# The first MLP matmul of seven chunks as seven half-size products, with g folded into w1, x's block sums on GpSimd and v cast by DMA into its operand

## The chip, the cores and the metric

The kernel runs on one core of a Trainium2 chip. The metric is the device time of one execution in microseconds (us); lower is better. The engines are named as in the profile: PE (TensorE, matmuls), PEld (its weight loads), DVE (VectorE), ACT (ScalarE), POOL (GpSimd), SP (SyncE, which here only issues DMAs).

## What is computed

Linear attention over 8 batches of 8 heads, 576 rows and 64 columns, followed by a layer norm and a two-layer MLP with a residual. Cut to what matters:

```python
q_s = softmax(q, axis=-1)              # over the 64 columns of a head
k_s = softmax(k, axis=2)               # over the 576 rows
kv  = einsum('bhsd,bhse->bhde', k_s, v)
x   = einsum('bhsd,bhde->bhse', q_s, kv)   # heads side by side: (8, 576, 512)
xn  = (x - mean(x)) / sqrt(var(x) + 1e-6) * g_ln
out = x + relu(xn @ w_ch1) @ w_ch2     # w_ch1 512 x 2048, w_ch2 2048 x 512
```

All inputs and the output are float32.

## The kernel before

**Chunks.** The 4608 rows are worked off as nine chunks of 512. Chunks 0 to 7 hold rows 0 to 511 of each batch; chunk 8 (`C9`) holds the last 64 rows of all eight batches. For one chunk, PE computes `mm1` (xn times w1, 2048 hidden columns, then relu into `hT`) and `mm2` (`hT` times w2).

**Order.** The program is in a manual schedule: each engine executes its instructions in the order in which the Python code issues them. `run(main, side)` (L677) walks the matmul steps of a chunk's MLP, each with a weight, and issues a side job as soon as the sum of the weights has reached the job's position. So everything that belongs to the next chunks (attention, exponentials, loads, transposes) has a position within the current chunk: 120 units in chunks 2 to 7 (64 for mm1, 56 for mm2).

**mm1.** `mlp_steps` (L648) gives a chunk above 1 first 32 matmuls of 256 columns (`mm1_part`, L429: the first four blocks of w1, for one half of the chunk's rows and then the other), then 48 matmuls of 512 columns (`mm1`, L414). A block of 128 hidden columns needs four matmuls, one for each 128 of the 512 input columns (`KO1` = 4). ACT applies the relu from PSUM into `hT` (L402, L439).

**mm2** of chunks 1 to 8 (`mm2_fast`, L598) is already computed as seven half-size products: both operands are cut into 2 x 2 blocks and combined by sums and differences. `sum_h` (L494, instructions at L505, DVE) forms four sums S of hT's blocks (`hs`) in two groups; `quarter_w2` (L481, DVE) formed four differences T of w2's blocks (`w2_q`) in chunks 0 and 1. Each product is 16 matmuls of 256 columns (`prod`, L521). Partial results stay in PSUM banks `a`, `b`, `c`, `e`: ACT copies one (`copy_u`, `seed_c`, L546, L619), DVE adds one (`add_u`, L549). `y_quarter` (L532, DVE) scales by the row's 1/sigma and adds the residual, and POOL's DMA queue stores the result (L538).

**PSUM.** Pool `mm_ps` has six banks for all of mm1 and mm2; pool `att_ps` has two for attention. A new tile takes the bank that was released longest ago in program order, and its first writer waits for the last reader of the old tile.

**Attention of the next chunk** (`attn_fast`, L744) lies within the current one: `reduce_q` (L199) sums the exponentials of q; `kv_mm` (L259, 20 short matmuls) multiplies exp(k) with v, with a column of ones beside every pair of heads for the denominator; DVE normalises into `kv_sb` (L268); `po_mm` (L291, 16 short matmuls) gives x. `x_fast` (L338) scales x and accumulates its row sum, L344 turns the sum into minus the mean, and `xn_out` (L331) computes (x - mean) times g, with g in a tile that is repeated over all partitions. ACT's `square_sum` (L325) gives the variance, which is applied only at the end (`rstd_op`). `xn_T` (L207) transposes two quarters of xn by a DMA from SP's queue into `xnT`, mm1's moving operand: quarters 0 and 1 first, quarters 2 and 3 at position 101 of 120.

**Preparation** (`prep_fast`, L731): two chunks ahead, SP's queue loads q, k, v (1 MB each, in runs of 1 KB), and ACT computes the exponentials (L183, L149). v arrives as float32 and is cast by ACT into `vm` (L157) for batches 3 to 7; for batches 1 and 2 the DMA casts it to bf16 and DVE copies it (L159). The last 64 rows go to `vtr` and are cast by DVE into `vr` (L166). POOL's queue has the weights and the first loads at the start, and the stores from then on.

Chunk 8's attention (`attn_rest`) lies in chunk 7. Its MLP comes last, with `last_products` in place of `mm2_fast`'s list, and nothing beside it.

Of the kernel before, what the change touches and what calls it, by code (L numbers as in the profile page):

```python
# [20 lines left out]
def kernel(  # L21
# [30 lines left out]
    VW = P + 2  # L52
# [7 lines left out]
    const = ctx.enter_context(tc.tile_pool(name="const", bufs=1))  # L60
    raw = ctx.enter_context(tc.tile_pool(name="raw", bufs=2))
# [18 lines left out]
    w1_sb = const.tile([P, KO1, DH], BF16)  # L80
# [4 lines left out]
    vr = const.tile([P, 2, NP, VW], BF16)  # L85
    vm = const.tile([P, 2, T, NP, VW], BF16)

# [19 lines left out]
    def alloc_kv(b):  # L107
        raws[b][0], raws[b][1], raws[b][3], raws[b][4] = (
            raw.tile([P, H, T, D], FP32, tag="kt", name="kt", bufs=1),
            raw.tile([P, H, T, D], BF16 if b in CAST else FP32, tag="vt", name="vt", bufs=1),  # L110
            raw.tile([P, H // 2, D], FP32, tag="ktr", name="ktr"),
            raw.tile([P, H // 2, D], FP32, tag="vtr", name="vtr"),
        )
# [8 lines left out]
    def load_kvrem(eng, b):  # L122
        for src, dst in ((k, raws[b][3]), (v, raws[b][4])):
            for half in range(2):
                eng.dma_start(
                    dst[SR * half : SR * half + SR],
                    src[b, 4 * half : 4 * half + 4, SM:S, :].transpose([1, 0, 2]),
                )
# [13 lines left out]
    eks, eqs, eqTs, xs, xnTs, rstds = {}, {}, {}, {}, {}, {}  # L142

    def exp_k(b, j, hn=2):
        kt = raws[b][0]
        if j == 0:
            eks[b] = att.tile([P, T, H, D], BF16, tag="ek", name="ek")
        hs = slice(2 * j, 2 * j + hn)
        nc.scalar.activation(  # L149
            eks[b][:, :, hs, :].rearrange("p t h d -> p h t d"), kt[:, hs], AF.Exp  # L150
        )

    def cast_v(b, j, eng=None):
        hs = slice(2 * j, 2 * j + 2)
        dst = vm[:, b % 2, :, j, 0:P].rearrange("p t (h d) -> p h t d", h=2)
        if eng is nc.scalar:
            nc.scalar.copy(dst, raws[b][1][:, hs])  # L157
        else:
            nc.vector.tensor_copy(out=dst, in_=raws[b][1][:, hs])  # L159

    def prep_kvrem(b):
        par = b % 2
        nc.scalar.activation(ekr[:, par], raws[b][3], AF.Exp)
        for half in range(2):
            ps = slice(SR * half, SR * half + SR)
            nc.vector.tensor_copy(  # L166
                out=vr[ps, par, 2 * half : 2 * half + 2, 0:P],
                in_=raws[b][4][ps].rearrange("p (j h) d -> p j (h d)", h=2),
            )

    def new_eq(c):
        eqs[c] = (
            att.tile([P, T, H, D], BF16, tag="eq", name="eq"),
# [24 lines left out]
    def reduce_q(c, t):  # L198
        nc.vector.reduce_sum(eqs[c][1][:, t], eqs[c][0][:, t], axis=AX.X)  # L199
# [19 lines left out]
    def exp_k0(j):  # L219
        hs = slice(2 * j, 2 * j + 2)  # L220
        if j == 0:
            eks[0] = raw.tile([P, T0, H, D], BF16, tag="vt", name="ek0", bufs=1)
# [23 lines left out]
    def kv_mm(b, j, t):  # L246
# [5 lines left out]
        w = P + 1  # L252
        if b == 0:
            lhsT, rhs, w = k0_mm(j, t)
        elif t < T:
            lhsT, rhs = eks[b][:, t, 2 * j : 2 * j + 2, :], vm[:, par, t, j, 0 : P + 1]
        else:
            lhsT, rhs = ekr[:, par, 2 * (j % 2) : 2 * (j % 2) + 2, :], vr[:, par, j, 0 : P + 1]
# [4 lines left out]
        if j % 2 == 1 and t == last:  # L263
            js = slice(j - 1, j + 1)
            rzk = recip_z(pkv[:, :, P]) if b else kvbox["rz", j // 2]
            for half in range(2):
                ps = slice(64 * half, 64 * half + 64)
                nc.vector.tensor_mul(  # L268
                    kv_sb[ps, b, js, ps], pkv[ps, :, ps],
# [3 lines left out]
    def start_x(c):  # L273
# [3 lines left out]
            mlp.tile([P, T, DM], BF16, tag="xn", name="xn"),  # L277
# [45 lines left out]
    def square_sum(c, t):  # L323
        x, _, _, mv = xs[c]
        nc.scalar.activation(  # L325
            scrap, x[:, t], AF.Square, bias=mv[:, t, 0:1], accum_out=mv[:, t, 1:2]
        )

    def xn_out(c, t):
        x, _, xn, mv = xs[c]  # L330
# [4 lines left out]
    def x_fast(c, t):  # L335
# [6 lines left out]
            accum_out=st[:, t, 0:1],  # L342
        )
        nc.vector.tensor_scalar_mul(out=mv[:, t, 0:1], in0=st[:, t, 0:1], scalar1=-1.0 / DM)  # L344
        xn_out(c, t)

    def x_rest(t):
# [3 lines left out]
            scrap, x[:, t], AF.Copy, scale=-1.0 / DM, accum_out=mv[:, t, 0:1]  # L351
# [37 lines left out]
    def rstd_op(c):  # L389
# [4 lines left out]
            lnv, mv[:, :, 1], AF.Ln, bias=eps_ln, scale=1.0 / DM  # L394
# [14 lines left out]
    def mm1(c, m, ko):  # L409
        if m == 0 and ko == 0:  # L410
            new_h()
        if ko == 0:
            hbox["ph"] = mm_ps.tile([P, T, P], FP32, tag="m", name="ph")
        nc.tensor.matmul(  # L414
            hbox["ph"], w1_sb[:, ko, m * P : (m + 1) * P], xnTs[c][:, :, ko, :],
# [5 lines left out]
    def mm1_part(c, m, t0, tn, ko):  # L421
# [4 lines left out]
        if m % 2 == 0 and at == 0 and ko == 0:  # L426
# [3 lines left out]
            ph[:, m % 2, at : at + tn], w1_sb[:, ko, m * P : (m + 1) * P],  # L430
# [120 lines left out]
    def last_products(product):  # L551
# [32 lines left out]
        product(1, "a", first=True, at={  # L584
# [13 lines left out]
    def mm2_fast(c):  # L598
# [3 lines left out]
        def product(n, name, first=False, at=None, ts=range(2), own=False):  # L602
            at = at or {}
            for t in ts:
                for k in range(KH):
                    i = t * KH + k

                    def go(t=t, k=k, i=i):
                        if i == 0 and first:
                            bank(name)  # L610
                        prod(n, name, t, k, first or own, own)
                        for fn in at.get(i, []):
                            fn()

                    steps.append((0.5, go))
# [16 lines left out]
        def sums(*which):  # L632
            return [lambda g=g, i=i: sum_h(g, i) for g, i in which if g or c == FAST]

        late = c == FAST
        product(1, "a", first=True, at={
            0: sums((1, 0), (0, 1), (1, 1)) + ([] if late else sums((1, 2), (1, 3))), 15: [seed_c]})
        product(5, "b", first=True, at={8: sums((0, 2), (1, 2)) if late else []})
        product(6, "a", at={8: sums((0, 3), (1, 3)) if late else [], 15: [lambda: copy_u("s2")]})
# [7 lines left out]

    def mlp_steps(c):  # L648
        full = range(KO2)
# [4 lines left out]
        else:  # L654
            full, parts = range(4, KO2), ((0, 0, 2), (0, 2, 2))
            if c == 1:
                full, parts = range(8, KO2), ((0, 0, 2), (1, 0, 2), (0, 2, 2), (1, 2, 2))
# [39 lines left out]
    def prep_side(b, a0, a1, sums=True):  # L697

        n = a1 - a0
        s = spread([lambda j=j: exp_q(b, j) for j in range(NP)], a0, a0 + 0.4 * n)  # L700
        s += [(a0 + 0.4 * n, lambda: (prep_kvrem(b), eq_T(b)))]
        s += spread([lambda j=j: exp_k(b, j) for j in range(NP)], a0 + 0.5 * n, a1)
        s += spread([lambda j=j: cast_v(b, j) for j in range(NP)], a0 + 0.1 * n, a0 + 0.5 * n)
        if sums:
            s += spread([lambda t=t: sum_q(b, t) for t in range(T)], a0 + 0.5 * n, a1)
        return s

    def attn_side(c, kv0, kv1, po0, po1, pe=None):


        s = []
        if c < B:
            s += spread(
                [lambda j=j, t=t: kv_mm(c, j, t) for j in range(NP) for t in range(T + 1)],
                kv0, kv1,
            )
        fns = []
        for t in range(T):
            fns += [lambda t=t, i=i: po_mm(c, t, i) for i in range(NP - 1)]
            fns.append(lambda t=t: (po_mm(c, t, NP - 1), x_out(c, t)))  # L720
        s += [(po0, lambda: start_x(c))] + spread(fns, po0, po1)
        if pe:
# [339 lines left out]
```

## Time and profile before

| what | value |
|---|---|
| median of 3 runs | 280.28 us (280.23 to 280.35) |
| span of the profiled execution, first to last instruction | 279.2 us |
| PE busy in it | 273.3 us |
| DVE, ACT, POOL busy | 195.2, 181.9, 36.8 us |
| DMA moved | 48.01 MB in 68844 packets |
| granted clock of PE | full in every slice |
| idle of PE between 60 us and 270 us | none that the table of windows shows |

The page gives the profiled execution by its span alone; the runs' times are about 1.1 us above it (280.28 - 279.2 = 1.08), the part ahead of the first instruction and behind the last. The chain of waits is read from its end backwards: each piece is what had to end for the next one to start. Busy times of DVE and ACT are unions: where two instructions overlap by their pipelines, the time counts once. A single ACT or DVE instruction on 512 columns is recorded with some 0.6 to 0.7 us, and back to back they start some 0.5 to 0.6 us apart.

### The profile page before, as it was taken

Reading aid. Unit: us, or ns where it says so; the run is one execution under the profiler, and the core shown is the slowest. Engines: PE = TensorE matmul, PEld = TensorE weight load, DVE = VectorE, ACT = ScalarE, POOL = GpSimd, SP = SyncE. Lnnn points to the kernel's source line nnn. Section 1 sums busy time; section 2 is a strip of 40 time slices with the busy share of each in tenths; the row PEclk is TensorE's granted clock in tenths of the full one; section 3 lists DMA queues with packets and bytes.
Section 4 is the critical chain, followed back from the end, with each engine's and each line's share of the span. In section 5 each row is a group of like instructions: output and inputs, shape, how many; then the busy total and the mean of one; then the engine's idle time right before and its main releaser. Section 6 shows DMA issues by size and latency. Waiting matters only on the chain.

```text
span 279.2 us, 5666 instructions
## 1 busy us (share of the span) xinstructions
PE 273.3 (98%) x2245; PEld 202.1 (72%) x2245; DVE 195.2 (70%) x457; ACT 181.9 (65%) x346; POOL 36.8 (13%) x64
## 2 busy tenths in 40 slices
PE   8999999999999999999999999999999999999994
PEld 6888855766995589558955896589658855885683
DVE  4573647987996688658865886588657929962363
ACT  4568871797987785678668766876585477526500
POOL 3922224200030003000300030003000300030000
PEclk9999999999999999999999999999999999999999
DMA  7999999799969995994499469544914410241014
GB/s 182 245 207 207 336 218 332 172 256 308 193 155 348 285 173 156 320 230 90 132 328 238 95 146 290 133 75 121 219 38 79 126 65 1 40 122 66 2 38 113
DMA packets 68844, 48.01 MB, mean 172 GB/s; under 512 B 40401, under 2 KB 65489, under 8 KB 68818
## 3 DMA queue, kind: packets, MB, share of 16 engines
q1 hardware_dynamic: 57074, 27.66, 42.7%
q0 software_dynamic: 11152, 19.47, 27.7%
q10 hardware_dynamic: 592, 0.52, 0.6%
q8 instruction: 17, 0.28, 0.4%
q14 instruction: 9, 0.07, 0.1%
HBM read 36.70 MB, written 9.44 MB: 165 GB/s over the span
## 4 chain that ended last, share of the span: by engine, by line
PE 90%; DMA 5%; DVE 2%; POOL 1%; issue 0%; DVEq 0%
PE ph L414 28%; PE ba L521 20%; PE ph L429 15%; PE bb L521 5%; PE bc L521 5%; PE be L521 5%; PE pc L474 4%; DMA w_sb<-in_moe_w_ch_dram 4%; PE pkv L259 3%; PE po L291 2%; DMA qt<-in_q_dram 2%; PE ptr L803 1%; PE po L298 1%; DVE xn L331 1%; POOL v L866 1%; DVE x L338 1%
## 5 line engine op out<-in xcount | busy, mean ns | idle before, releaser
L414 PE MATMUL ph<-xnT,w_sb 128*128 128x512 bf16 x368 | 87.2, 379 | 0.0
L402 ACT ACTIVATE hT<-ph 128x512 bf16<-128x512 f32 x92 | 53.5, 598 | 18.4 <-PE ph L414 18.4
L414 PEld LDWEIGHTS <-w_sb 128*128 128x128 bf16 x368 | 34.0, 98 | 34.5 <-issue 0.2
L521 PEld LDWEIGHTS <-hs 128*128 128x128 bf16 x512 | 49.1, 98 | 5.8 <-DVE hs L505 0.2
L429 PE MATMUL ph<-xnT,w_sb 128*128 128x256 bf16 (+1 forms) x432 | 52.7, 269 | 0.3 <-DMA w_sb<-in_moe_w_ch_dram 0.3
L439 ACT ACTIVATE hT<-ph 128x512 bf16<-128x512 f32 x48 | 28.6, 600 | 24.5 <-PE ph L429 24.3
L429 PEld LDWEIGHTS <-w_sb 128*128 128x128 bf16 x432 | 38.4, 98 | 4.3 <-DMA w_sb<-in_moe_w_ch_dram 0.5
L505 DVE TENSOR_TENSOR hs<-hT 128x1024 bf16<-128x1024 bf16 x32 | 21.9, 687 | 27.8 <-ACT hT L402 27.6
L521 PEld LDWEIGHTS <-hT 128*128 128x128 bf16 x384 | 36.6, 98 | 5.2 <-ACT hT L402 0.2
L538 POOL DMA_DIRECT2D out_dram<-ot x28 | 15.0, 541 | 179.8 <-DVE ot L532 155.9
L521 PE MATMUL ba<-w_q,hs 128*128 128x256 bf16 x256 | 31.3, 273 | 0.0
L331 DVE SCALAR_TENSOR_TENSOR xn<-x,mv,g_bc 128x512 bf16<-128x512 bf16 x34 | 25.5, 751 | 1.2
L338 DVE SCALAR_TENSOR_TENSOR x<-po,rq 128x512 bf16<-128x512 f32 x30 | 20.6, 686 | 6.5 <-PE po L291 6.1
L325 ACT ACTIVATE scrap<-x,mv 128x512 bf16<-128x512 bf16 x34 | 24.6, 724 | 0.1
L291 PE MATMUL po<-kv_sb,eqT 128*128 128x128 bf16 x128 | 24.1, 219 | 0.2 <-DVE kv_sb L268 0.2
L199 DVE TENSOR_REDUCE zq<-eq 128x8 f32<-128x512 bf16 x32 | 20.1, 686 | 4.1 <-ACT eq L191 2.4
L259 PE MATMUL pkv<-vm,ek 128*128 128x129 bf16 x112 | 21.2, 220 | 0.0
L546 ACT COPY s<-ba 128x512 f32<-128x512 f32 x15 | 8.8, 584 | 16.7 <-PE ba L521 16.7
L291 PEld LDWEIGHTS <-eqT 128*128 128x128 bf16 x128 | 11.7, 98 | 7.5 <-issue 0.6
L521 PE MATMUL ba<-w_sb,hT 128*128 128x256 bf16 x128 | 16.2, 273 | 0.0
L474 PE MATMUL pc<-w_sb,hT 128*128 128x512 bf16 x64 | 15.9, 379 | 0.0
L521 PE MATMUL bb<-w_q,hs 128*128 128x256 bf16 x128 | 15.8, 273 | 0.0
(117 smaller groups left out, 340.2 us busy)
## 6 DMA issues: line engine op xcount, KB each, us to landing
out_dram<-ot POOLq DMA_DIRECT2D x32, 256.0 KB, 3.0
qt<-in_q_dram SPq DMA_DIRECT2D x5, 1024.0 KB, 7.5
kt<-in_k_dram SPq DMA_DIRECT2D x5, 1024.0 KB, 6.9
vt<-in_v_dram SPq DMA_DIRECT2D x5, 1024.0 KB, 10.9
w_sb<-in_moe_w_ch_dram POOLq DMA_DIRECT2D x8, 512.0 KB, 14.0
qt<-in_q_dram POOLq DMA_DIRECT2D x2, 1024.0 KB, 15.9
kt<-in_k_dram POOLq DMA_DIRECT2D x2, 1024.0 KB, 15.9
kt<-in_k_dram SPq DMA_DIRECT2D x4, 288.0 KB, 5.9
```

Source lines behind the costliest of these rows:

```text
L259: nc.tensor.matmul(pkv[:, j % 2, 0:w], lhsT, rhs, start=(t == 0 and j % 2 == 0), stop=(t == last), skip_group_check=True,)
L291: nc.tensor.matmul(pobox["p"][:, i * P : i * P + P], eqTs[c][:, t, i, :], kv_sb[:, c, i, :], start=True, stop=True,)
L325: nc.scalar.activation(scrap, x[:, t], AF.Square, bias=mv[:, t, 0:1], accum_out=mv[:, t, 1:2])
L331: nc.vector.scalar_tensor_tensor(xn[:, t], in0=x[:, t], scalar=mv[:, t, 0:1], in1=g_bc, op0=ALU.add, op1=ALU.mult)
L338: nc.vector.scalar_tensor_tensor(x[:, t].rearrange("p (h d) -> p h d", h=H), in0=pobox[c, t].rearrange("p (h d) -> p h d", h=H), scalar=1. ...
L402: nc.scalar.activation(dst, src, AF.Relu)
L414: nc.tensor.matmul(hbox["ph"], w1_sb[:, ko, m * P : (m + 1) * P], xnTs[c][:, :, ko, :], start=(ko == 0), stop=(ko == KO1 - 1),)
L429: nc.tensor.matmul(ph[:, m % 2, at : at + tn], w1_sb[:, ko, m * P : (m + 1) * P], xnTs[c][:, t0 : t0 + tn, ko, :], start=(ko == 0), stop=( ...
L439: nc.scalar.activation(dst, ph, AF.Relu)
L474: nc.tensor.matmul(hbox["pc", t], hbox["h"][:, ko, t, :], w2_sb[:, ko, :], start=(ko == 0), stop=(ko == KO2 - 1),)
L505: nc.vector.tensor_tensor(out=dst, in0=x, in1=y, op=op)
L521: nc.tensor.matmul(hbox[bank][:, t], lhsT, rhs, start=first and (own or t == 0) and k == 0, stop=k == KH - 1, skip_group_check=True)
```

## The change

Seven parts go together.

1. **mm1 of chunks 2 to 8 (`c > FAST`) as seven products** (`mm1_fast`, `prod1`, new). w1's and xn's blocks are cut 2 x 2 (even and odd blocks of 128 hidden columns by two halves of the input columns; two halves of the rows). For each of four groups of four hidden blocks, seven products of four matmuls of 256 columns replace eight. Partial results go through PSUM tiles `x`, `b`, `c`: ACT copies two (`seed`, `copy_5`), DVE adds two (`add_5`, `out_22`), ACT applies three relus, and DVE takes the maximum with zero for the fourth block in SBUF, for two groups at once. The groups go in pairs, slot by slot.
2. **g folded into w1**: `scale_w1` (DVE, eight instructions in chunk 0) writes `w1g` = w1 times g; chunks 1 to 8 use it. g as a column comes from four tiny matmuls and one DVE instruction in `first_batch`. `xn_out` becomes a tensor_scalar of 512 x minus the row sum, without g and without L344; the factor 512 is taken out again in `square_sum` and `rstd_op`. Chunk 0 keeps the old form.
3. **w1's block sums**: `sum_w1` (DVE, sixteen instructions of 128 x 512) in chunks 0 and 1, into the memory of the raw w1.
4. **x's block sums**: `sum_x`, eight instructions of 128 x 256 for each chunk, on POOL for chunks 2 to 7 and on DVE for chunk 8; they need both halves of `xnT`.
5. **v**: for batches 3 to 7 `load_v` issues from POOL's queue four casting DMAs straight into `vm` (runs of 64 numbers: 256 bytes read, 128 written) and two into `vr`. `vm` gets a column of ones beside every head instead of every pair. Casts L157 and L166 go. Batches 1 and 2 keep a staged tile.
6. **Buffers**: `ek` and `eq` have one buffer instead of two; the first batch's `ek` lies in `kt`'s memory.
7. **Positions**: a chunk above 1 has 112 units now (56 and 56), and nearly every side job is moved: exponentials and square sums lie in mm2, kv_mm at 4 to 28, po_mm at 48 to 75, the second `xn_T` at 78, `sum_x` at 84 to 100, `reduce_q` in two double-size instructions within the chunk before. In mm2, some products take their matmuls in another order (`cut`).

```diff
+    def load_v(b):
...
+        for t in range(0 if b in CAST else T):
+            nc.gpsimd.dma_start(vm[:, b % 2, t, :, 0:D], src[:, t])
...
+    def sum_x(c, i):
...
+        dst, x, y = ((t1, b12, b11), (t2, b22, t1), (t3, b22, b12), (t4, b21, t2))[i]
+        eng = nc.gpsimd if c < C9 else nc.vector
+        for t in range(2):
+            eng.tensor_tensor(out=dst[:, t], in0=x[:, t], in1=y[:, t], op=ALU.subtract)
...
     def xn_out(c, t):
+        nc.vector.tensor_scalar(
+            out=xn[:, t], in0=x[:, t], scalar1=float(DM), scalar2=mv[:, t, 0:1],
+            op0=ALU.mult, op1=ALU.subtract,
+        )
...
+    def mm1_fast(c):
...
+        def seed(g):
+            at[g, "c"] = mm_ps.tile([P, 2, 2, P], FP32, tag="m", name="bc")
+            nc.scalar.copy(at[g, "c"], at[g, "x"])
+        def copy_5(g):
+            nc.scalar.copy(at[g, "s"], at[g, "b"])
+        def add_5(g):
+            nc.vector.tensor_tensor(out=at[g, "b"], in0=at[g, "x"], in1=at[g, "s"], op=ALU.add)
+        def out_22(g):
+            nc.vector.tensor_tensor(
+                out=h_out(g, 1, 1), in0=at[g, "x"], in1=at[g, "s"], op=ALU.add
+            )
+            if g % 2:
+                dst = hbox["h"][:, 4 * g - 3 : 4 * g + 4 : 2, 2:4, :]
+                nc.vector.tensor_scalar_max(dst, in0=dst, scalar1=0.0)
...
+        def slot(g, n):
+            if n == 0:
+                product(1, g, "x", True, [lambda: seed(g)])
+                product(5, g, "b", True, [lambda: copy_5(g)])
+            elif n == 1:
+                product(6, g, "x", False, [lambda: add_5(g)])
+                product(2, g, "c", False, [
+                    lambda: out_relu(g, "c", 0, 0, nc.scalar)])
+            elif n == 2:
+                product(7, g, "x", False, [lambda: out_22(g)])
+                product(3, g, "b", False, [lambda: out_relu(g, "b", 0, 1, nc.scalar)])
+            else:
+                product(4, g, "x", False, [lambda: out_relu(g, "x", 1, 0, nc.scalar)])
+        for g0 in (0, 2):
+            for n in range(4):
+                for g in (g0, g0 + 1):
+                    slot(g, n)
...
     def mlp_steps(c):
+        if c > FAST:
+            return mm1_fast(c) + mm2_fast(c)
...
-        s += [(60, lambda: xn_T(c, 0, 2)), (101, lambda: xn_T(c, 2, 2)), (105, lambda: rstd_op(c))]
+        s += [(61, lambda: xn_T(c, 0, 2)), (78, lambda: xn_T(c, 2, 2)), (95, lambda: rstd_op(c))]
+        s += spread([lambda i=i: sum_x(c, i) for i in range(4)], 84, 100)
...
+        return s + spread([lambda i=i: sum_x(C9, i) for i in range(4)], 102, 104)
...
+                        side += [(30, lambda b=c + 3: load_v(b))]
```

## The prediction

> **What bounds the kernel now.** I read the page's busy times, then the windows of two steady chunks, then the chain of waits. The page:
>
> ```profile
> PE 273.3 (98%) x2245; PEld 202.1 (72%) x2245; DVE 195.2 (70%) x457; ACT 181.9 (65%) x346; POOL 36.8 (13%) x64
> ```
>
> A share is a mean, so I cut the span where chunks 3 and 4 begin and end. Columns: stretch, length, busy time of PE, PEld, DVE, ACT, POOL, clock, DMA share, GB/s.
>
> ```profile
> 108.64:136.75 28.11, 28.11 (x231) 20.82 (x229) 20.83 (x50) 20.27 (x38) 1.75 (x4) 1.00 0.80 198
> 136.75:164.85 28.10, 28.10 (x230) 20.81 (x229) 20.83 (x50) 20.28 (x38) 2.54 (x5) 1.00 0.82 198
> ```
>
> PE has no gap: a chunk lasts as long as its matmuls. The chain of waits through the undisturbed last chunk (start, us, what) prices them:
>
> ```profile
> 249.12 3.49 PE ph L429 x32
> 252.61 10.36 PE ph L414 x48
> 262.97 1.75 PE ba L521 x16
> ```
>
> A matmul of 512 columns costs 10.36 / 48 = 0.216 us, one of 256 columns 1.747 / 16 = 0.109, in mm1 as in mm2.
>
> **PE's term.** mm1 now: 3.49 + 10.36 = 13.85 us. After: 7 products x 4 groups x 4 matmuls = 112 x 0.109 = 12.23. That is 1.62 less, in seven chunks 11.3. The rest of a steady chunk, 12.23 for mm2 and 2.03 for attention, stays (130 instead of 129 columns in kv_mm is nothing). The floor is a span of 279.2 - 11.3 = 267.9 and a chunk of 26.49. What I must find is how much of 11.3 comes back as waits.
>
> **DVE and ACT, by the chunk.** DVE's rows of chunk 4 (count, busy us, mean ns, idle before), then two rows of the whole trace:
>
> ```profile
> L331 DVE SCALAR_TENSOR_TENSOR xn<-x,mv,g_bc 128x512 bf16<-128x512 bf16 x4 | 3.0, 752 | 0.1
> L344 DVE TENSOR_SCALAR mv<-st 128x1 f32<-128x1 f32 x4 | 0.6, 154 | 0.1
> L166 DVE CAST vr<-vtr 64x256 bf16<-64x256 f32 x2 | 0.6, 284 | 0.0
> L549 DVE TENSOR_TENSOR be<-bb,s 128x512 f32<-128x512 f32 x1 | 0.7, 699 | 0.8 <-ACT s L546 0.8
> ...
> L159 DVE COPY vm<-vt 128x512 bf16<-128x512 bf16 x8 | 1.8, 288 | 3.3 <-DMA vt<-in_v_dram 3.3
> L437 DVE TENSOR_SCALAR hT<-ph 128x512 bf16<-128x512 f32 x4 | 2.8, 691 | 6.5 <-PE ph L429 6.5
> ```
>
> Added: four add_5 and four out_22 at 0.70 (L549) = 5.6. The two maxima, 1024 numbers in SBUF, have no row of their kind: two copies L159 give 0.58, two L437 1.38; I take 0.58 (bf16 in SBUF on both sides), 1.2 together. Gone: L344 0.6, L166 0.6. xn as tensor_scalar costs between 0.29 (L159) and 0.69 (L437) instead of 0.75; I take 0.29, which saves 1.9. Net +3.7, to 24.5 of 26.5 (93%); the upper ends make 20.8 + 5.6 + 2.8 - 1.2 - 0.2 = 27.8, above PE's floor. Back to back, DVE instructions start 0.60 apart instead of 0.70 (L505 at 98.08, 98.68, 99.28), so the lower figure is the likelier. ACT exchanges 16 relus for 12 relus and 8 copies (0.60 and 0.58) and loses four casts L157 (0.61): 20.3 - 0.1 of 26.5. So neither replaces PE as the bound, but DVE has little left, and its order now matters: add_5 and out_22 stand in DVE's queue behind kv_sb, sum_h and x_fast, and PE waits for them.
>
> **The new waits inside mm1.** A piece (four matmuls of one product) is 0.437 us. DVE starts 0.20 us after PE's last slot (L532 at 108.68, slot end 108.48), takes 0.70, and PE follows 0.05 later (kv_sb ends 45.98, po 46.03): 0.95. add_5 and the first group's out_22 have three pieces, 1.31: covered by 0.36. The second group's out_22 has only two before p4 writes `x`: 0.95 - 0.87 = 0.08 of wait. In the first pair, 20 kv_mm stretch the slots and cover that. In the second pair sum_h (0.60 each at positions 39 and 42) stands ahead: out_22 starts up to 0.65 late, less the 0.36 and the 0.22 of four po_mm. I take 0.25 a chunk for chunks 2 to 7 (bounds 0 and 1), 1.5 in all, and 0.5 for chunk 8, which has no attention beside it. ACT's `seed` of the second group starts 0.3 us after its p1 ends (0.20, and 0.1 behind copy_5), takes 0.58, and p6 writes `x` 1.31 after: covered by 0.4. PSUM: by order of release, the next pair takes the banks of c, c, b, b, x, x, all read long before. At a chunk's start p5 of the second group takes mm2's bank `a`, free about 1.1 us after p4's end, needed at 1.31: covered, unless DVE is late.
>
> **Where DVE is late.** sum_x of chunk 8 runs on DVE at 102 to 104 of chunk 7, ahead of its last y_quarters. Eight at 0.35 (half of L505's 0.69; bounds 0.2 and 0.69) is 2.8 us; DVE now idles 1.3 there (before L549 at 246.28 and L532 at 247.41). So bank `a` is free about 2.5 after p4, 1.2 too late; 1.0 taken (0 to 3).
>
> **POOL.** Its trace shows no tensor_tensor. Nearest rows: affine_select of 128 columns 0.29, twice for 256 columns 0.58; DVE's 1024 columns 0.69. I take 0.6 for each, 4.8 for eight (bounds 1.6, at 0.20 for the memset of 128 columns, and 11, at twice the 0.69). [...] Cover: xn_T at 78 of 112 goes out some 6.6 us before the chunk's end (x_fast of quarter 3 leaves DVE 1 us late), lands in 3.1 (median in the row of xnT, 8.3 at most), so the first two sums are done 2.3 us before the end and the last 1.3 after; p5 needs the first 0.4 after the start, p4 the last 5.2 after. In chunk 1, POOL also issues v for batches 3 and 4 (six DMAs of 0.89 or 0.63 each), and earlier in the trace each POOL DMA waits 1.4 to 2.9 us for older ones. 0.5 taken once (0 to 2.5).
>
> **DMA.** v as 4096 runs of 256 bytes instead of 1024 of 1 KB. Queue q1's packets take 0.427 x 16 x 279.2 / 57074 = 33 ns, q0's 0.277 x 16 x 279.2 / 11152 = 111. 4096 x 33 / 16 = 8.4 us; before, 1024 packets at 33 to 111 (70 taken) = 4.5. The share rises from 0.81 x 28.1 = 22.8 us to 26.7 of 26.5: full while batches 3 to 6 load. v itself has one and a half chunks of lead, k three quarters; what a full DMA delays is xn_T.
>
> **Hidden or small.** scale_w1 (8 x 0.58, upper 1.4) lies in chunk 0 where DVE waits 4.2, 1.0 and 1.05 us for PE ahead of L437; sum_w1 (16 x 0.35) half where DVE waits 3.3 for v, half in chunk 1, which loses as much by L344, L331 and L166; without that cover, up to 1 us. The matmuls for g's column stand before z0: 4 at 0.16 (zs) to 0.3, but PE then waits 0.35 for w1 at 18.07; 0.2 taken (-0.3 to 0.8, chunk 1's own waits included). Single `ek` and `eq` buffers: the last reader is done by position 28 or in the chunk before, the next writer comes at 57.
>
> **Sum.** 267.9 + 1.5 + 0.5 + 1.0 + 0.5 + 0.2 = 271.6 of span. The runs stand 1.1 above the span (280.28 - 279.2): **272.7 us**.
>
> **Rivals.**
> 1. *PE's floor*: order and pipelining cover all waits. 267.9 + 1.1 = 269.0, to 270.4. For it: no gap in six chunks today. Against: DVE at 93%. 0.20.
> 2. *DVE becomes the bound*: xn or the maxima run at the upper ends, or DVE loses time to what POOL now does in SBUF; a chunk of 27.5 instead of 26.5 gives back 7 of the 11.3 and with the other waits about 276 to 279.7. For it: 27.8 above. 0.13.
> 3. *Slower, by late sums of x*: DMA is full, xn_T lands in 8.3 us (the longest now) instead of 3.1, POOL needs 1.2 for two sums: the first is ready 8.3 + 1.2 - 6.6 = 2.9 us after the chunk's start, and p5, needing it at 0.4, waits 2.5 in each chunk. It decides from 1.62 a chunk (landing above 7.4). Price 7 x 2.5 = 17.5 against 11.3: 285 to 287. Against it: from chunk 5 on the DMA share is 0.60 and less. 0.14.
> 4. *It doesn't do what it says*: copies and adds stop PE between slots in each pair by 0.8, so that the products cost what the matmuls cost; about 280, within 0.2%. 0.03.
>
> Forecast (270.4 to 276): 0.50. Faster by over 0.2%: 0.83; within 0.2% (about what a measurement here can tell from no change): 0.03; slower: 0.14. The range leaves out rival 3 and part of 4 and reaches from 0.2 under the floor (chunk 1's wait gone) to the end of rival 2: 268.8 to 279.7.
>
> **What would show it.** mm1's matmuls in the chain: 112 of 0.109 in 12.2 to 12.7 us; a chunk of 26.5 to 27. PE's waits for DVE at p4, at the start of chunk 8, and nowhere for POOL. xn as tensor_scalar near 0.29; POOL's sums near 0.6 and done before the chunk's start plus 2. Wrong, if PE waits for `tq` or for `w1q`, or if DVE is busy over 25.5 of a chunk.

## The result, and the profile after

The changed kernel takes **283.17 us** (median of 5 runs, 282.05 to 284.36) against 280.28 before: 1.0105 times as long, interval 1.0077 to 1.0133. The forecast was 272.7, in 268.8 to 279.7. The profiled execution is the 284.36 us run, with a span of 282.6 us; the forecast's own span was 271.6, so 11.0 us have to be explained. The runs of this kernel lie further apart than those of the kernel before because PE's clock is not granted in full everywhere (mean 0.982 to 0.988), which is part of the story; the profiled run is one of the two at 0.982, the median run has 0.988. In what follows a median is taken over all runs of a kernel and a ratio over those within 1.5% of its fastest, so the two can differ.

The page's first line no longer shows PE at 98%:

```profile
PE 269.2 (95%) x2477; PEld 227.3 (80%) x2477; DVE 225.2 (80%) x495; ACT 185.6 (66%) x354; POOL 91.3 (32%) x142
```

The windows of chunks 1, 3 and 4 (columns as in the prediction: stretch, length, busy PE, PEld, DVE, ACT, POOL, granted clock, DMA share, GB/s):

```profile
53.84:89.34 35.50, 30.92 (x251) 23.27 (x249) 25.72 (x57) 24.57 (x47) 15.33 (x22) 0.90 1.18 177
116.20:142.97 26.77, 26.77 (x263) 23.96 (x260) 23.77 (x52) 20.39 (x38) 12.04 (x19) 1.00 0.96 185
142.97:169.74 26.77, 26.77 (x263) 23.97 (x260) 23.77 (x52) 20.39 (x38) 12.04 (x19) 1.00 1.03 186
```

Chunks 3 and 4 are what was forecast: 26.77 us instead of 28.10, and PE without a gap. Chunk 1, in which the change replaces no matmul at all, lasts 35.50 us; before it lasted 28.44, all of it busy PE at full clock:

```profile
51.93:80.37 28.44, 28.44 (x251) 22.51 (x249) 25.71 (x64) 25.27 (x49) 2.54 (x5) 1.00 0.84 216
```

PE's waits of the whole trace, longest first (total, times, longest):

```profile
PE po L342 <- DMA eqT<-eq: 4.6, 1, 4.6
PE ba L589 <- ACT s L614: 1.1, 1, 1.1
PE warm L850 <- DVE junk L976: 1.1, 1, 1.1
PE po L349 <- DVE x L358: 0.8, 1, 0.8
PE bx L733 <- DVE hT L767: 0.7, 2, 0.5
```

The 1.1 at `junk` was there before. The `eqT` line is in chunk 1: `po` of chunk 2 waits for the DMA transpose of that chunk's exponentials of q. In the chain of waits it is one piece of 11.45 us:

```profile
59.24 0.03 ACT hT L507
59.27 11.45 DMA eqT<-eq
70.72 0.05 issue
70.76 0.29 PE po L342
71.05 0.43 PE ph L482
71.48 0.21 PE po L342 x2
71.69 0.43 PE ph L482
```

`PE ph L482` shows the second cost: 0.43 for one matmul of 512 columns, where it was 0.216. The windows behind the wait give the clock (last three columns: granted clock, DMA share, GB/s):

```profile
66.00:69.00 3.00, 0.19 (x1) 0.00 (x0) 1.64 (x4) 0.61 (x2) 3.00 (x4) 0.91 1.59 169
69.00:72.00 3.00, 1.24 (x6) 0.69 (x7) 0.00 (x0) 0.00 (x0) 0.75 (x2) 0.50 1.25 258
72.00:75.00 3.00, 3.00 (x12) 1.35 (x11) 1.65 (x4) 1.10 (x2) 0.00 (x0) 0.50 1.57 211
75.00:78.00 3.00, 3.00 (x24) 1.91 (x23) 2.39 (x8) 1.71 (x4) 0.00 (x0) 0.95 2.09 138
```

PE stands for 4.6 us (66.2 to 70.8) and then runs some 4.5 us, up to 75.3, at half rate. The same clock appears once more, at the start of the kernel, with no long wait ahead of it:

```profile
14.00:16.00 2.00, 2.00 (x22) 2.00 (x20) 0.58 (x2) 0.63 (x1) 0.00 (x0) 0.50 1.26 212
16.00:18.00 2.00, 2.00 (x19) 1.60 (x17) 0.89 (x3) 0.09 (x1) 0.89 (x1) 0.68 1.22 201
```

Read off where PE starts each chunk, the two profiled executions divide like this (the last column sorts the terms of the prediction into the stages):

| stage | before, us | after, us | difference | forecast |
|---|---|---|---|---|
| start to chunk 1 | 51.93 | 53.84 | +1.91 | +0.2 |
| chunk 1 | 28.44 | 35.50 | +7.06 | +0.5 |
| chunks 2 to 6 | 140.54 | 133.94 | -6.60 | -6.85 |
| chunk 7 and mm1 of chunk 8 | 41.90 | 42.71 | +0.81 | -1.49 |
| mm2 of chunk 8 and the end | 16.39 | 16.61 | +0.22 | 0 |
| span | 279.2 | 282.6 | +3.4 | -7.6 |

So the products do what they should in five chunks; the gain is lost at three places, and most of it in chunk 1. The 1.91 us at the start belong to the profiled run: four later kernels with the same start, whose profiles show no dip there (runs 2, 5, the first kernel of 4 and the one of 7 with the sums on POOL), begin chunk 1 at 51.4 to 51.5 us.

### The profile page after: what moved, and what is told of

It reads as the page before. It is cut to its first block, busy times and chain, and to the rows that moved or that the text cites. A ratio compares the mean times of both kernels' runs of the same rounds, so it can differ in the third digit from the quotient of the medians.

```text
span 282.6 us, 6420 instructions
## 1 busy us (share of the span) xinstructions
PE 269.2 (95%) x2477; PEld 227.3 (80%) x2477; DVE 225.2 (80%) x495; ACT 185.6 (66%) x354; POOL 91.3 (32%) x142
## 4 chain that ended last, share of the span: by engine, by line
PE 81%; DVE 10%; DMA 5%; ACT 1%; issue 1%; DVEq 0%; ACTq 0%
PE ba L589 17%; PE bx L733 16%; PE bb L733 8%; PE ph L497 5%; PE pc L542 4%; PE bb L589 4%; PE be L589 4%; PE bc L589 4%; DMA eqT<-eq 4%; PE bc L733 4%; PE warm L850 4%; PE pkv L308 3%; PE po L342 2%; DVE x L358 2%; PE ph L482 2%; DVE hs L573 2%
## 5 line engine op out<-in xcount | busy, mean ns | idle before, releaser
L733 PEld LDWEIGHTS <-w_q 128*128 128x128 bf16 x448 | 41.1, 98 | 5.0 <-issue 0.8
L248 POOL TENSOR_TENSOR tq<-xnT 128x256 bf16<-128x256 bf16 x24 | 15.5, 663 | 91.0 <-DMA xnT<-xn 91.0
L733 PEld LDWEIGHTS <-w1g 128*128 128x128 bf16 x336 | 31.3, 98 | 5.9 <-issue 2.1
L733 PE MATMUL bx<-tq,w_q 128*128 128x256 bf16 x224 | 35.1, 273 | 0.2 <-DVE bb L764 0.2
L764 DVE TENSOR_TENSOR bb<-bx,s 128x512 f32<-128x512 f32 x28 | 19.5, 698 | 12.7 <-ACT s L761 6.6
L210 DVE TENSOR_REDUCE zq<-eq 128x16 f32<-128x1024 bf16 (+1 forms) x20 | 20.7, 1050 | 4.9 <-ACT eq L201 2.5
L779 ACT ACTIVATE hT<-bc 128x512 bf16<-128x512 f32 x28 | 16.7, 597 | 9.0 <-PE bc L733 8.5
L308 PE MATMUL pkv<-vm,ek 128*128 128x130 bf16 x112 | 21.3, 220 | 0.0
L147 POOL DMA_DIRECT2D vm<-in_v_dram x20 | 17.7, 904 | 7.6 <-PE pkv L308 7.1
L767 DVE TENSOR_TENSOR hT<-bx,s 128x512 bf16<-128x512 f32 x28 | 18.6, 687 | 0.8 <-PE bx L733 0.4
L342 PEld LDWEIGHTS <-eqT 128*128 128x128 bf16 x128 | 12.1, 101 | 7.4 <-DMA eqT<-eq 5.1
L733 PE MATMUL bb<-xnT,w_q 128*128 128x256 bf16 x112 | 17.8, 273 | 0.0
## 6 DMA issues: line engine op xcount, KB each, us to landing
w_raw<-in_moe_w_ch_dram POOLq DMA_DIRECT2D x4, 512.0 KB, 12.3
```

The lines of the kernel that those rows point to most:

```text
L147: nc.gpsimd.dma_start(vm[:, b % 2, t, :, 0:D], src[:, t])
L210: nc.vector.reduce_sum(eqs[c][1][:, ts], eqs[c][0][:, ts], axis=AX.X)
L308: nc.tensor.matmul(pkv[:, j % 2, 0:w], lhsT, rhs, start=(t == 0 and j % 2 == 0), stop=(t == last), skip_group_check=True,)
L342: nc.tensor.matmul(pobox["p"][:, i * P : i * P + P], eqTs[c][:, t, i, :], kv_sb[:, c, i, :], start=True, stop=True,)
L733: nc.tensor.matmul(dst[:, q], lhsT, rhs, start=first and q == 0 and ko == 0, stop=ko == 1, skip_group_check=True)
L764: nc.vector.tensor_tensor(out=at[g, "b"], in0=at[g, "x"], in1=at[g, "s"], op=ALU.add)
```

## The experiments

**Theory** at the start: in chunk 1 POOL now issues v of batch 3, 4096 runs of 256 bytes. They lie beside eq's transpose, which lands 11.4 us after its issue instead of 7.8; `po` is also asked for about 1 us earlier (position 49 instead of 55); the long idle of PE then costs half a clock. The two landings (median us from issue to landing, of one transpose each), first in the kernel before:

```profile
eqT<-eq SPq DMA_TRANSPOSE x1, 7.8
eqT<-eq SPq DMA_TRANSPOSE x1, 11.4
```

**Rivals**: the earlier demand alone; the small size of the packets alone; a clock that dips for reasons of its own.

**1. v later, by position.** In `second_side`:

```diff
-        s += [(12, lambda: load_v(3)), (60, lambda: load_v(4))]
+        s += [(44, lambda: load_v(3)), (60, lambda: load_v(4))]
```

> The changed kernel with one edit: the loads of v for batch 3 go out at position 44 of chunk 1 instead of 12, so that their 256-byte packets are not in the queues while eq of chunk 2 is transposed by DMA. My theory (the small packets make the transpose land 3.6 us later, 11.4 instead of 7.8 us after its issue, and the long idle of PE then costs half a clock for 5 us): the transpose lands in 7.5 to 8.5 us, PE's wait at po of chunk 2 falls from 4.6 to 1 to 1.5, no half clock behind it, 6 us less than the changed kernel's 283.2, about 277. Rival A (po of chunk 2 is only demanded 1.2 us too early, and the transpose would be as late without v): PE still waits 4 us or more, 282.5 to 283.5. Rival B (the packets only move: they now stand in the way of xn_T of chunk 2): eqT is early, but PE waits for xnT at the start of chunk 2 or POOL for it, 279 to 283.

Measured: 284.28 us, 1.0132 (1.0078 to 1.0186); the wait is 4.8, the landing 11.72. Taken as it stands this speaks for rival A. POOL's timeline (start, length, instruction) says that the edit did not do what it says:

```profile
55.51 0.92 POOL L147 DMA_DIRECT2D vm<-in_v_dram  x1
56.69 2.65 POOL L147 DMA_DIRECT2D vm<-in_v_dram  x3 [0.26 <-PE ph L497]
```

In the changed kernel the same instructions start at 55.92 and 57.10. A position fixes the order on one engine's queue and nothing more: POOL had next to nothing to wait for in front of the load (0.26 us), so it ran ahead of PE.

**2. The demand later.** `kv` of chunk 2 goes from 37-45 to 43-53, `xn_T` from 58 and 77 to 63 and 80, and:

```diff
-        for t, (p0, p1) in enumerate(((49, 51), (55, 58), (62, 65), (70, 74))):
+        for t, (p0, p1) in enumerate(((55, 58), (60, 63), (66, 69), (74, 78))):
```

> The changed kernel with one edit: kv, po and xn_T of chunk 2 stand later in chunk 1 (kv at 43 to 53 instead of 37 to 45, the first po at 55 instead of 49, the last at 74 to 78 instead of 70 to 74), v of batch 3 stays at 12. My theory (3.6 us of the wait come from v's packets, 1.2 from the earlier demand): the transpose still lands in about 11.4 us, PE's wait falls from 4.6 to 3.4, and as that is close to the length of idle time behind which the half clock came, the half clock may or may not come; 279.5 to 282. Rival A (the earlier demand is all of it): the wait goes, 277. Rival B (neither; PE's half clock has a cause of its own): 283.

Measured: 283.13 us, 1.0059 (1.0025 to 1.0093). The wait is still 4.3: the transpose landed 12.28 us after its issue this time and ate the later demand. Rival A is out; the size was missed. The median is also the 283 that rival B named, so this run alone doesn't tell the theory from it; runs 3 and 4 do.

**3. v into the kernel before** (the converse). `second_side` of the kernel before gets, at position 12:

```diff
+        for t in range(T):
+            nc.gpsimd.dma_start(vx[:, t], src[:, t])
...
```

(and likewise two DMAs for the last 64 rows).

> The converse, on the kernel before: at position 12 of chunk 1 POOL also issues the six casting DMAs of v of batch 3 in 256-byte runs, into memory that nobody reads (0.6 MB of extra reading, no other edit; the kernel's own loads stay). My theory: eqT of chunk 2 lands about 3.6 us later than its 7.8, PE waits about 3.5 us at po of chunk 2 and perhaps runs at half clock behind it: 283.5 to 286.5 against 280.28. Rival (v's packets do not delay the transpose): 280.2 to 280.6.

Measured: **287.35 us, 1.024** (1.0192 to 1.0288). Six DMAs that nobody reads, and the kernel before shows the whole picture: the transpose lands in 12.1 us (7.8 without them), PE waits 4.1, and the clock is 0.50 from 69 to 75 us. The median is 0.85 above the upper end of what was expected. The landing and the windows behind it:

```profile
eqT<-eq SPq DMA_TRANSPOSE x1, 12.1
69.00:72.00 3.00, 2.66 (x10) 1.28 (x11) 0.70 (x3) 0.60 (x1) 0.00 (x0) 0.50 1.31 291
72.00:75.00 3.00, 3.00 (x14) 1.58 (x13) 1.45 (x3) 1.77 (x4) 0.00 (x0) 0.50 1.14 360
```

**4. v really held back.** A write by DVE into v's target makes POOL wait (v goes out from 65.83 us instead of 55.92):

```diff
+    def late_v3():
+        nc.vector.memset(vm[0:1, 1, 0, 0, 0:1], 0.0)
+        load_v(3)
-        s += [(12, lambda: load_v(3)), (60, lambda: load_v(4))]
+        s += [(50, late_v3), (110, lambda: load_v(4))]
```

> The changed kernel with the loads of v really held back: a DVE memset of one number of their target at position 50 of chunk 1 makes POOL wait for it (a later position alone moved nothing, because POOL runs ahead of PE), and v of batch 4 follows at 110. My theory (the 256-byte packets delay the transpose): the transpose of eq of chunk 2 lands in 7.5 to 8.5 us instead of 11.4, PE's wait falls from 4.6 to 1 to 1.5, no half clock behind it in chunk 1, chunk 1 lasts 29 to 30 instead of 35.5 us; 276 to 278. Rival A (the wait has another cause): no change, 283. Rival B (late packets now delay xn_T of chunk 2, issued at 58 and 77): a wait for xnT or tq early in chunk 2 of 2 us or more, 279 to 282.

Measured: 279.62 us, 0.9974 (0.9941 to 1.0007); five of its ten runs have a clock of 0.997 or more, and these take 277.7 to 279.2. The transpose lands in 6.8 us, the wait for it is gone from the list, and chunk 1 lasts 28.7 us:

```profile
eqT<-eq SPq DMA_TRANSPOSE x1, 6.8
```

Rival B came true elsewhere: the longest wait is now `PE bb L733 <- POOL tq L248`, 1.9 us at the start of chunk 3. On SP's queue the *issue* of eq's transpose of chunk 4 takes 4.75 us there (1.55 in the changed kernel) beside v of batch 5, and xn's second transpose stands behind it.

The same kernel with g's column by DMA (the edit is shown in 7):

> As the kernel before this one in the list (v held back), and in addition g's column comes by DMA and no small matmuls stand ahead of z0. If these matmuls cause the dip of the clock at 14 to 18 us, no execution of this kernel shows it (clock 0.995 or more in all runs) and its median lies 1 to 2 us below the other's, 275 to 276.5, with runs less far apart. If the dip has nothing to do with them: same median within 0.5 us and dips in some runs of both.

Measured: 281.34 us, 1.0039 (1.0013 to 1.0065). It doesn't tell what it was meant to: the wait for `tq` at chunk 3 is 2.4 us here, and in the profiled run the clock falls behind it (0.55 on average from 112 to 115 us), with a full clock at the start. That may be why nine of ten runs have a clock of 0.994 or less; the other traces weren't kept.

**5. The same bytes in larger runs.** v of batch 3 at its place in the changed kernel, but staged in runs of 1 KB:

```diff
-    CAST = (1, 2)
+    CAST = (1, 2, 3)
+        s += [(80 + 2 * j, lambda j=j: cast_v(3, j)) for j in range(2)]
```

> The changed kernel with v of batch 3 issued at the same place, but into a staging tile in runs of 1 KB (1024 packets instead of 4096, the same bytes), copied into the operand by two DVE casts at 80 and 82 of chunk 1. Theory as it stands (the number of small packets is what delays the transpose): eqT lands in 8 to 9 us, the wait falls below 2, 276.5 to 280. Rival (the bytes or the queue do it, not the packets' size): eqT at 11 us or more, 283 or more.

Measured: 282.26 us, 1.0039 (1.0015 to 1.0063), and a landing of 10.8 us, between the two expectations and nearer the rival's. What lay in the queues in the eight us from 2 us after the issue (packets, MB, share of 16 DMA engines; q0 is POOL's queue, q1 SP's), first in the changed kernel, then with 1 KB runs, then with v held back:

```profile
q0 software_dynamic: 4595, 0.58, 112.1%
q1 hardware_dynamic: 2387, 0.85, 62.2%
```

```profile
q1 hardware_dynamic: 2293, 0.79, 72.8%
q0 software_dynamic: 1584, 0.59, 64.6%
```

```profile
q1 hardware_dynamic: 3687, 1.93, 109.6%
```

With a third of the packets and the same bytes SP's queue still moves only 0.79 MB in the time in which it moves 1.93 with POOL's queue empty, and the landing gains 0.6 of 3.6 us. So the number of small packets is not the main thing: what POOL's queue holds beside the transpose slows it, in larger packets too (10.8 us here, 7.8 in the kernel before).

**6. v early, and the clock at the start.** Two kernels with v of batch 3 in chunk 0 (position 103) and the sums of x of chunk 8 on POOL; the first also has the small matmuls for g's column inside mm1 of chunk 0 (position 22), the second leaves them ahead of z0.

```diff
-        s += [(12, lambda: load_v(3)), (60, lambda: load_v(4))]
+        s += [(60, lambda: load_v(4))]
+            + [(103, lambda: load_v(3))]
-        eng = nc.gpsimd if c < C9 else nc.vector
+        eng = nc.gpsimd
+            + [(22, g_column)]
```

> The changed kernel with three edits: v of batch 3 is issued in chunk 0 ahead of that chunk's output stores (position 103), so that its packets have landed when eq of chunk 2 is transposed; the small matmuls for g's column stand inside mm1 of chunk 0 (position 22) and not ahead of z0; the sums of x of chunk 8 on POOL. My theory: eqT of chunk 2 lands in 8 us or less, PE's wait at po is 1 us or less, chunk 1 lasts 29 to 30 us (35.5 in the changed kernel), no wait for tq at chunk 3, clock 0.995 or more in nearly all runs: 274 to 276.5, below the kernel before. Rival A (v's packets now collide with other loads of chunk 0 and eqT is late again): 281 or more. Rival B (the dips of the clock have nothing to do with PE's idle time and the small matmuls): median like the next kernel's, with dips in as many runs.

> As the kernel before this one in the list, but with the small matmuls for g's column left ahead of z0 as in the changed kernel. My theory: in 3 to 5 of 10 runs the clock is lower (0.994 or less) and the time 2 us longer, the other runs as fast as its neighbour's; median 0.3 to 2 us higher. Rival: no difference between the two beyond 0.3 us.

Measured: 282.82 us, 1.0033 (1.0003 to 1.0063), and 283.63 us, 1.0103 (1.0088 to 1.0118). Rival A: in the first kernel POOL stood still for 1.5 us (1.51 to 1.56) ahead of each of three of v's DMAs, so that v was out only at 55.7 (56.3 in the second), and chunk 0's output stores (1 MB), issued behind them, slid to 55.7 to 57.9 (56.3 to 58.7 in the second kernel), onto the transpose, which landed in 11.4 and 9.8 us. The stores are large runs, but v of batch 4 went out from 63.3 and 65.6 us, while the transpose was still under way, so these two kernels don't show the stores' part alone. All five runs of the second kernel have a clock of 0.982 or less, and its trace has the half clock at the start; the first kernel's trace has not, though eleven of its twelve runs are at 0.994 or less as well.

**7. Parts done alone.** g's column by a DMA in the changed kernel, with the lines of the matmuls removed; these lines put ahead of z0 in the kernel before; the sums of x of chunk 8 on POOL. The first edit:

```diff
-            nc.tensor.matmul(
-                gcp[:, ko : ko + 1], g_row[:, ko * P : ko * P + P], ones_f[:, 0:1],
-                start=True, stop=True,
-            )
+            nc.sync.dma_start(
+                g_in, bass.AP(moe_g_ln.tensor, moe_g_ln.offset, [[1, P], [P, KO1], [1, 1]])
+            )
```

> The changed kernel with one edit: the column of g for scale_w1 comes by a small DMA in chunk 0 and not from four matmuls of a 1-row operand ahead of z0. My theory (these small fp32 matmuls leave PE nearly idle for a microsecond ahead of z0 and kv of chunk 0, and the clock of 0.50 to 0.68 granted at 14 to 18 us comes from that): first mm1 matmul at 18.1 to 18.5 instead of 19.9, clock 1.00 at 14 to 18 us, 281.2 to 281.6 against 283.2. Rival (the dip at the start falls into some executions of any kernel): same dip, less than 0.5 us gained, all of it the matmuls' own time.

> The kernel before with the small matmuls for g's column and their DVE scaling at the place where the changed kernel has them, result unused. My theory: about 0.3 us of their own, and in some executions the clock falls to half at 13 to 17 us, 1.5 to 2 us more: median 281 to 282.5, runs further apart than those of the kernel before. Rival (the dip needs something else of the change): 280.3 to 280.8, clock 0.995 or more in all runs.

> The changed kernel with the block sums of x of chunk 8 on POOL as in the other chunks. My theory (these eight instructions stand ahead of the last outputs on DVE, so the PSUM bank and the first sums of chunk 8 come late): the waits at the start of chunk 8 and in its mm1 (13.17 for 12.23 of matmuls) shrink by 0.5 to 1.2 us; the rest of chunk 7 and the wait in chunk 1 stay. Total 282 to 282.7 if the start is as in the changed kernel's run. Rival (POOL at 0.66 each is later than DVE at 0.23 to 0.28): chunk 8 starts no earlier or its products wait for tq, no change or up to 1 us more.

Without the matmuls: 283.24 us, 1.0099 (1.0067 to 1.0130). The trace has a full clock at 14 to 18 us, as expected, the first mm1 matmul at 17.5 (19.9 in the changed kernel's profile) and chunk 1 at 51.2. The median doesn't gain: chunk 1's wait was 4.9, and the changed kernel's own median run, at 0.988, need not have the dip. In the kernel before: 280.74 us, 1.0037 (1.0011 to 1.0063); six of ten runs take 280.3 to 280.8 at a clock of 0.997 or more, one 281.7 at 0.994, three 282.7 to 282.9 at 0.992; of 26 runs of the kernel before beside them one is below 0.997 (four of all its 84 runs beside the experiments, each at 0.994). The sums on POOL: 282.48 us, 1.0094 (1.0053 to 1.0135); chunk 7 and mm1 of chunk 8 take 42.35 instead of 42.71. Only 0.36, below what was expected: the wait for `ot` at the start of chunk 8 is gone, the rest is elsewhere.

**8. No products in mm1 of chunks 7 and 8.** The first kernel of 6, without sums of x for chunk 8, `sum_h` at the positions of the kernel before, and:

```diff
-        if c > FAST:
+        if FAST < c < B - 1:
             return mm1_fast(c) + mm2_fast(c)
```

> As the first kernel of this list, but mm1 of chunks 7 and 8 as in the kernel before (full-size matmuls, no sums of x for chunk 8): the products stay in chunks 2 to 6 alone. By PE's matmuls alone it would lose 2 x 1.62 = 3.2 us. My theory (DVE bounds chunk 7 with add_5, out_22 and the maxima beside the work for chunk 8, so that the products cost there more than they save: 42.7 us for the two chunks against 41.9 before): 0.4 to 1.2 us faster than its neighbour. Rival (the products pay in chunks 7 and 8 too, other things make chunk 7 long): 1.5 to 3.2 us slower.

Measured: 283.36 us, 1.0089 (1.0055 to 1.0122). Its chunk 7 and mm1 of chunk 8 take 42.96, those of the first kernel of 6 42.37: the products gain 0.6 there, not 3.2, and don't lose. Both sides missed. With full-size matmuls chunk 7 still takes 29.1 us where it took 28.0 before, so its new order of chunk 8's attention costs 1.1 by itself (`po` waits 0.7 there for `x` from DVE).

**9. All repairs together.** v held back as in 4, the sums of x of chunk 8 on POOL, and two positions: eq's transpose of chunks 4 and later behind xn's second one, and one `x_rest` of chunk 7 behind the copy of `s` that PE waited 1.1 us for:

```diff
-... (70, lambda: eq_T(b))]
+... (82, lambda: eq_T(b))]
-... (69, 77, 79, 82))
+... (69, 77, 79.6, 82))
```

The first of four kernels has the small matmuls inside mm1, the second ahead of z0, the third none (DMA), the fourth is the third with the second half of w1's sums in chunk 0 at 94 to 97.

> The changed kernel with v of batches 3 and 4 held back (as in the gated kernel, 277.7 us in its undisturbed runs), eq's transpose of chunks 4 and later issued at 82 instead of 70 (behind xn's second one on SP), the sums of x of chunk 8 on POOL, the small matmuls for g's column inside mm1 of chunk 0, and one x_rest of chunk 7 behind the copy that PE waits for. My theory (waits for DMA transposes and the half clock behind them are what was missed; small matmuls ahead of z0 cause the dip at the start): no wait of PE over 1.2 us, clock 0.995 or more in nearly all runs, 274.5 to 277, faster than the kernel before by 1 to 2%. Rival (the rest of the change gains less than its matmuls say, because DVE bounds chunk 1 and others): 278 to 280 with full clock.

> As the kernel before this one, with the small matmuls for g's column ahead of z0 as in the changed kernel. My theory: in 3 to 7 of 10 runs the clock is at or below 0.994 and the time 1.5 to 2.5 us longer; the others equal the neighbour. Rival (the dip has another cause): as many low-clock runs in both, medians within 0.3 us.

> The kernel with v held back and the matmuls ahead of z0, but with g's column by a small DMA in chunk 0 and no such matmuls. My theory (the dip at the start belongs to these matmuls): clock 0.996 or more in nearly all runs, median 274.5 to 275.5, as the other's undisturbed runs (274.9). Rival (the dip falls on any kernel with these waits): low clock in a third of the runs or more, median 276 or more.

> As the kernel before this one, with the second half of the sums of w1 (eight DVE instructions of 0.67 us between starts for two) in chunk 0 at 94 to 97 instead of in chunk 1 at 30 to 64. My theory (DVE bounds chunk 1 and these sums are the surplus): chunk 1 is 0.7 to 1.2 us shorter, chunk 0 at most 0.3 longer; 0.5 to 1 us below its neighbour. Rival (they fill gaps in chunk 1, or they delay kv and po of chunk 1 in chunk 0 as much): no difference beyond 0.3 us, or slower.

| kernel | median, us | ratio to before, interval | runs with a clock of 0.994 or less |
|---|---|---|---|
| matmuls inside mm1 | 277.23 | 0.9883 (0.9864 to 0.9902) | 1 of 5 |
| matmuls ahead of z0 | 276.35 | 0.9836 (0.9800 to 0.9873) | 3 of 6 |
| column by DMA | 276.52 | 0.9857 (0.9835 to 0.9879) | 0 of 5 |
| and w1's sums early | 276.82 | 0.9889 (0.9849 to 0.9929) | 0 of 6 |

All four beat both kernels. The waits of the second (its profile is one of the runs with the dip at the start):

```profile
PE warm L850 <- DVE junk L980: 1.1, 1, 1.1
PE bb L733 <- DVE qt L1078: 0.9, 1, 0.9
PE po L349 <- DVE x L358: 0.8, 1, 0.8
PE bx L733 <- DVE hT L767: 0.7, 2, 0.5
PE bb L733 <- POOL tq L248: 0.3, 1, 0.3
```

Its chunk 1 lasts 28.71 us and its chunk 7 28.28: the one ACT step, 0.6 positions later, gains 1.27 of 29.55 (the sums on POOL alone left it at 29.54). Its three runs at full clock take 274.9 to 275.1. The low-clock runs came about as often as expected in the first three, but the expected medians were met by none: inside mm1 the small matmuls, meant to be harmless, put the end of chunk 0 at 53.04 instead of 51.35 in the third kernel; and the third and fourth keep waits of their own (2.2 us for `tq` at chunk 3; 1.4 us of `pkv` for v's cast, which now stands behind w1's sums on DVE). In the fourth, chunk 1 is 28.59 instead of 28.79 and chunk 0 35.24 instead of 33.71, so the sums of w1 are not what fills DVE there: its rival holds.

## Why the prediction was wrong

**The floor and the products: right.** Chunks 2 to 6 gain 6.60 of the 6.85 forecast, a chunk is 26.77 (26.5 to 27 named), and nowhere in them does PE wait for `tq` or `w1q`. DVE is busy 23.8 us of a chunk (24.5 forecast). Of the 0.25 a chunk taken for `out_22`, 0.16 can be read, though the profile counts no gap: the 16 matmuls `bx<-tq,w1g`, which write `x` behind it, take 1.91 from start to start where 16 others take 1.75. `po` takes 0.14 more than before (1.03 for 0.89). DVE's rows in chunk 4 and POOL's in the whole trace:

```profile
L764 DVE TENSOR_TENSOR bb<-bx,s 128x512 f32<-128x512 f32 x4 | 2.8, 698 | 1.9 <-ACT s L761 1.4 <-PE bx L733 0.6
L767 DVE TENSOR_TENSOR hT<-bx,s 128x512 bf16<-128x512 f32 x4 | 2.6, 686 | 0.0
L389 DVE TENSOR_SCALAR xn<-x,mv 128x512 bf16<-128x512 bf16 x4 | 1.4, 353 | 0.1
L772 DVE TENSOR_SCALAR hT<-hT 128x1024 bf16<-128x1024 bf16 x2 | 1.2, 578 | 0.1
```

```profile
L248 POOL TENSOR_TENSOR tq<-xnT 128x256 bf16<-128x256 bf16 x24 | 15.5, 663 | 91.0 <-DMA xnT<-xn 91.0
```

xn 0.35 (0.29 taken), the maxima 0.58 (0.58), POOL's sums 0.66 (0.6), `add_5` and `out_22` 0.70 and 0.69. That the maxima agree to the digit is luck: chunk 4's two took 0.73 and 0.43. Rival 2 also has DVE losing time to what POOL does in SBUF; no row showed that ahead of the result, and in the changed kernel's trace only three of the fourteen maxima are longer than 0.43 (0.73 to 0.74), beside POOL's issue of v's DMAs and not beside its sums.

**The DMA step: wrong, and the cause of most of it (6.6 of 11.0 us).** The prediction saw the share rise to 26.7 of 26.5 and went on: "what a full DMA delays is xn_T". It asked which *data* have lead, not which *transfer is in flight beside the new ones*. In chunk 1 that is eq's transpose, and its lead was nil: before, it landed at 65.19 and the first `po` began at 65.24. Runs 3, 4 and 5 show that traffic on POOL's queue beside it delays it by 3 to 5 us (12.1 us in run 3 and 10.8 in run 5, against 7.8) and that holding it back restores it (6.8 in run 4). The 7.06 divide into 4.6 of wait (3.6 from the later landing, 1.0 from the earlier demand) and about 2.5 of half clock behind it. The prediction priced chunk 1 at 0.5, for POOL's time to issue v; eq's transpose had no term in its sum. The mechanism is that of its rival 3, a late transpose, but of another tensor in another chunk, and once instead of seven times: from chunk 2 on, eq's transposes land in 4.3 to 4.4 us in the changed kernel.

**The half clock: not in the prediction.** In chunk 1 the profile shows 4.6 us of idle (66.2 to 70.8 us) and 0.50 from 68.5 to 75.3 us; in the nine other traces with such a wait there the clock is 0.50 for 3.4 or 6.8 us. The shortest waits with a half clock behind them are 2.9 us (second kernel of 6) and 2.4 us (second kernel of 4), 3.4 us of it each; behind 2.2 us (third kernel of 9) and 1.9 us (first of 4) there is none. What switches the clock, and when, no run here shows beyond these lengths. On the queues, the runs show that a second one slows the first (the transpose landed in 11.4 us beside v and in 6.8 with v held back, run 4); how the DMA engines divide their time between the two, they don't show.

**The start: the dip of the clock was left out (0.2 taken, 1.9 in the profile).** The four products for g's column were counted by their own length, and without the dip that holds: chunk 1 begins at 51.4 us with them (first kernel of 4) and at 51.2 without (first of 7), 51.9 in the kernel before. With them ahead of z0, and no long wait elsewhere, 7 of 16 runs (10 of the kernel before with them, 6 of the repaired one) have a clock of 0.994 or less; of the three repaired kernels without them there, 1 of 16. Of all traces kept, 4 of the 9 with them ahead of z0 have the half clock between 12 and 20 us, and none of the 9 others. That they raise the chance of the dip is likely by this; how they do it, no run shows.

**Chunks 7 and 8: mis-sized (-1.49 forecast, +0.81 measured).** The sums of x on DVE were priced at 1.0 and measured 0.36. What was left out is the order of chunk 8's attention on ACT and DVE: 1.27 from `x_rest` ahead of a copy that PE needs. In the changed kernel's profile PE stands still for 2.98 us in the two stretches (42.71 less 39.73 busy), where 1.75 were taken. After that repair the two still gain less than their matmuls say (0.8 of 3.2 us); this rest (`x` of chunk 8 late on DVE 0.8, `hT` 0.7) was not taken apart further.

**What would show it**: the points named held for chunk length, POOL and, nearly, xn (0.35); mm1 of chunk 8 took 13.16 instead of 12.2 to 12.7; and the point "wrong, if" named only `tq`, `w1q` and DVE. The repaired kernel's 274.9 at full clock is 2.2 above the forecast.

## What to carry to other kernels

For every transfer that a change adds, list the transfers already in flight in the same microseconds and look up the slack of each: the landing time against the first reader's start (65.19 and 65.24 us here), and not the share of DMA time in the chunk. Price a wait of some microseconds at more than itself: here 4.6 us of it were followed by 4.5 us of PE at a clock of 0.50. And expect the position of a load in a hand-written order to fix nothing but its place behind its own engine's instructions, unless something it must wait for is there: position 44 instead of 12 left v at 55.51 us (55.92 before), a write that POOL had to wait for moved it to 65.83.

## What the runs showed of the hardware

- Transfers on POOL's queue slowed a transpose issued by SP: eq's of chunk 2 landed in 5.0 to 7.9 us in the eight traces without v on that queue beside it and in 9.8 to 12.3 in the ten with it, whether in runs of 256 bytes alone or with 1 KB runs or output stores among them. In the changed kernel the time is lost behind the issue: the issue took 5.7 us in the kernel before and 5.8 in the changed one, the rest up to the landing 2.1 and 5.7.
- PE's clock fell to 0.50 in or just behind every wait of 2.9 to 5.1 us in chunk 1, in all ten traces of this study that have one: for 6.8 us in the five in which it fell before the wait's end, for 3.4 in the five in which it fell after it. Behind the one wait of 2.4 us it fell too, for 3.4 us; behind 2.2 and 1.9 it didn't (mean clock 0.997 in both of these runs).
- In the changed kernel the maximum of 1024 columns in SBUF took 0.43 us, but 0.73 to 0.74 in each of the three cases (96.0, 122.8, 149.6 us) in which POOL was issuing v's DMAs beside it. POOL's sums of x, which also read SBUF, lengthened no DVE instruction beside them that the trace shows (the outputs of L600: 470 to 485 ns in chunks 1 to 6, 473 to 479 in chunk 7, which has no such sums); none of these was a maximum or a sum of two operands in SBUF.
- The issue itself was slow at times: eq's transpose of chunk 4 held SP's queue for 1.5 us in the changed kernel and 4.8 beside v of batch 5 (run 4). But that of chunk 2 held it for 5.7 us in the kernel before, with no v on POOL's queue, so v's packets alone don't decide it.
